# Block-sparse attention and a two-layer MLP: value blocks in every fourth partition, score columns in block-minor order

## The chip, the cores and the metric

The kernel runs on one core of one Trainium2 chip. The metric is device time in microseconds (us): the median of three runs is 771.02, from 770.57 to 773.94. A core has five engines that run their own instruction queues: TensorE (PE in the profile, with weight loads as PEld), VectorE (DVE), ScalarE (ACT), GpSimd (POOL), and SyncE (SP), whose queue issues most DMAs here. Work meets in SBUF, which has 128 partitions, and in PSUM, where PE's results land in eight banks.

## The reference

Four batches, eight heads, 768 positions, head size 64. Positions form 24 blocks of 32. A query block sees the first and the last block, its own and its two neighbours, and three sampled blocks; the query blocks 0 and 23 see everything. The attention's output goes through an MLP with a squared relu.

```python
scores = scale * np.matmul(q, k.transpose(0, 1, 3, 2))
mask = np.abs(blk_i - blk_j) <= window
mask = mask | (blk_i == 0) | (blk_j == 0) | (blk_i == n_blocks - 1) | (blk_j == n_blocks - 1)
for qb in range(n_blocks):
    for kb in sampled_blocks[qb]:
        mask[qb * block:(qb + 1) * block, kb * block:(kb + 1) * block] = True
scores = np.where(mask, scores, -1000000000.0)
...
attn = attn / (np.sum(attn, axis=-1, keepdims=True) + 1e-09)
return np.matmul(attn, v).astype(np.float32)
...
h = x @ w_in
r = np.maximum(h, 0.0)
g = s * (r * r) + b
return (g @ w_out).astype(np.float32)
```

## The kernel before

The kernel has two stages. The attention comes first, the MLP follows on the same core, and the decoding of the MLP's weights (they arrive as 64-bit floats and are split into pairs of 32-bit ones) is spread over the late attention and the early MLP.

**Slots.** The attention runs as a list of slots (`T["ORD"]`, L31). A sparse slot is one query block of two batches with all eight heads: 44 of them, four units each, one unit for each batch and half of the heads. A dense slot has the two query blocks that see everything, for one batch and four heads: 8 of them, two units each. The order is four dense slots, then 18 sparse ones, then four dense ones woven in with sparse ones, then the rest.

**A sparse slot.** The keys are gathered in `keys_tile` (L873): for the slot's window three blocks and the first block, for its samples three blocks and the last one. GpSimd copies them there (`window_k`, `sampled_k`). `scores` (L931) issues 16 matmuls, each in two passes (32 records), on tiles of 64 rows and 32 columns, with the eight key blocks as 256 moving columns, block after block. `maximum` (L954) takes scores out of PSUM, adds a mask per block (`mt`, a column for each of eight blocks) and finds the row's maximum; `exp` (L969) makes exponentials and their sum. `transposes` (L995) turns two chunks of 128 columns, window and samples, so that keys lie on partitions, `evacuate` (L1008) copies them to SBUF, and `av` (L1051) multiplies with values.

**Values.** A value tile has 128 partitions: three blocks of 32 rows and a fourth for the first or last block, one below the other, because the transposed probabilities come out in that order. `window_v` (L769), `sampled_v` (L860) and `global_values` (L757) load them by DMAs of SP, 32 partitions for a block; adjoining blocks go together (`runs`, L747). Window values stay in three streams (A, B, C), in which each slot loads one new block over the oldest; sampled values go round in five places.

**A dense slot.** `scores_dense` (L919) makes 768 columns a unit in two halves of 384. Each half has a maximum (the second begins with the first's), an exponential over 384, four transposes of 96 columns, and an evacuation of 96 partitions to `dense_part` (L729). Where a sparse slot brings window blocks 3n, 3n+1, 3n+2 into a value tile, `av_dense` (L1032) uses their 96 partitions for the dense rows as well. `recip` (L981) adds the sums.

**Tiles that turn.** Probabilities use eight tiles `ptiles` (L287), scores and transposes share six PSUM banks (`next_bank`), `nm` and `dns` hold maxima and sums.

**The order.** `Plan` (L109) simulates the engines with given costs and due times and writes out each engine's order; L1149 to L1315 give it the operations of a slot with their dependences and buffers. PE's own order is a list (`line`, L1306): transposes of a slot, transposed outputs of the slot before, scores of the slot after the next, then the products with values.

Of the kernel before, what the change touches and what calls it, by code (L numbers as in the profile page):

```python
# [9 lines left out]
F32 = mybir.dt.float32  # L10
# [202 lines left out]
def kernel(  # L213
# [73 lines left out]
    ptiles = [cp.tile([P, HALF], F32, tag=f"p{n}", name=f"ptile{n}") for n in range(8)]  # L287
    ps = ctx.enter_context(tc.tile_pool(name="ps", bufs=1, space=PSUM))
# [372 lines left out]
    with ExitStack() as es:  # L661
# [66 lines left out]

        def dense_part(b, x, j, g):  # L729

            n = NCK // 2 * 4 * P
            if ("d", b) not in vbox:
                vbox[("d", b)] = gp.tile([P, 3 * n // 2], F32, tag=f"z{b % 2}", name=f"dp{b}", bufs=1)
            d = vbox[("d", b)]
            if g == 0:
                return d[:, :n].rearrange("p (c u q) -> p c u q", c=NCK // 2, u=4)[:CH, :, 2 * x + j]
            rest = pool("khp" if b % 2 == 0 else "klp")[1].bitcast(F32) if x else d[:, n:]
            return rest.rearrange("p (c u q) -> p c u q", c=NCK // 2, u=2)[:CH, :, j]
# [18 lines left out]
        def global_values(m):  # L757


            value_tiles()  # L760
            if m < 4:
                z, a = "AB"[m // 2], m % 2
                n, j = (NST, 0) if z == "A" else (4, NB - 1)
                nc.sync.dma_start(out=vbox[z][NSL * BLK:, :n, a, :], in_=v[a, j * BLK:(j + 1) * BLK, :].unsqueeze(1).broadcast_to([BLK, n, DM]))
            else:
                nc.sync.dma_start(out=sampled_values(0)[NSL * BLK:], in_=block_rows(0, NB - 1))
                holds["v"].update((row, 0) for row in range(VG))

        def window_v(i, entire, m):  # L769

            _, e, k, r = slots[i]
            rr = runs(k, entire)
            if m < len(rr):
                j, p, n = rr[m]
            else:
                j, p, n = 0, NSL, 1
            nc.sync.dma_start(out=window_values(r)[p * BLK:(p + n) * BLK], in_=block_rows(e, j, n))
# [3 lines left out]
        make_identity(nc, ident)  # L781
        warm = pers.tile([P, 1], F32, name="warm")
# [12 lines left out]
        nc.gpsimd.memset(mt[:, NB - 2, (NB - 1) % 3:(NB - 1) % 3 + 1], NEG)  # L795
# [26 lines left out]
        def sparse_sampled(G):  # L822
# [15 lines left out]
            G.tensor_scalar(out=mt[:, 1:NB - 1, 4:4 + NSL], in0=iv, scalar1=1.0, scalar2=NEG, op0=ALU.min, op1=ALU.mult)  # L838
# [21 lines left out]
        def sampled_v(i, a):  # L860
# [5 lines left out]
            if a == 0 and holds["v"].get(row) != e:  # L866
                holds["v"][row] = e
                nc.sync.dma_start(out=vt[NSL * BLK:], in_=block_rows(e, NB - 1))
# [50 lines left out]
        def scores_dense(i, k):  # L919

            _, b, x, _ = slots[i]
            n, qt, kt = unit_of[i], qts[q_of(i)], kts[b // 2]
            for par in range(2):
                sp = sps[(n + par, k)] = next_bank(f"s{n + par}_{k}")
                for a in range(2):
                    pair = 2 * x + a
                    nc.tensor.matmul(sp[halves[a], :HALF], qt[halves[par], b % 2, pair, halves[a]],
                                     kt[halves[par], k * NB // 2:(k + 1) * NB // 2, b % 2, pair * BLK:(pair + 1) * BLK],
                                     start=True, stop=True, tile_position=(par * D, a * D))

        def scores(i, a):  # L931
# [13 lines left out]
            for par in range(2):  # L945
                to = sps[(u + 2 * a + par, 0)]
                for pair in range(NPAIR):
                    o = (k - 1) % 4 * BLK if k <= 4 * NSP else pair % 2 * D + (k - 1) % 4 * BLK
                    nc.tensor.matmul(to[quads[pair]], qt[halves[par], a, pair, o:o + BLK], keys[halves[par], :, :, pair * BLK:(pair + 1) * BLK],  # L949
# [4 lines left out]
        def maximum(n, g):  # L954
            i, j = units[n]
            kind, b, k, _ = slots[i]
            if g == 0:
                nms[n] = sm.tile([P, 2], F32, tag="nm", name=f"nm{n}", bufs=10)
# [604 lines left out]
```

## Time and profile before

| | us |
|---|---|
| median of three runs | 771.02 |
| lowest, highest | 770.57, 773.94 |
| profiled execution, its own time | 772.56 |
| its span (first to last instruction) | 770.8 |
| granted clock of TensorE, mean | 0.987 |

The profile comes from one execution. Its page gives busy times by engine, the span in 40 slices, DMA queues, a chain of waits followed back from the last instruction, and the costliest groups of instructions. A line of a group reads: source line, engine, operation, written and read tiles, partitions x elements, count | busy time, mean ns of one | idle time of the engine just before, and what ended it. Line numbers are those of the kernel before. The dense groups of before, for instance, are L927 (scores), L966 with `mz` (maxima), L978 with 384 elements (exponentials), L1004 (transposes), and L1017 and L1019 with 96 partitions (evacuations); the sparse ones are L949, L966 with `mt`, L978 with 256, L1006, L1017 and L1019 with 128, L1058 (products with values).

### The profile page before, as it was taken

The page shows a single profiled execution, that of the slowest core. Times are in us where ns is not written, and L with a number is a line of the kernel's source. Part 1 is how long each engine was busy: PE and PEld are TensorE (multiplying, and loading weights), DVE is VectorE, ACT ScalarE, POOL GpSimd, SP SyncE. Part 2 cuts the span into 40 slices and gives each one's busy share as a digit, 9 for nine tenths or more (in the row PEclk, how much of TensorE's full clock was granted, in tenths as well). Part 3 has the DMA queues.
Part 4 walks back from the last instruction along what each step waited for, and adds up shares of the span by engine and source line. Part 5 has one row for each costly group of instructions (what it writes and reads, how often), then busy time and mean ns, then how long its engine had stood idle before and what let it go on. Part 6 is the DMA issues. An engine that isn't in the chain of part 4 may idle for free.

```text
span 770.8 us, 21373 instructions
## 1 busy us (share of the span) xinstructions
PE 733.4 (95%) x8032; PEld 620.6 (81%) x8032; DVE 562.9 (73%) x1433; ACT 473.0 (61%) x1141; POOL 242.1 (31%) x398
## 2 busy tenths in 40 slices
PE   8799787999898999999989999999999999999997
PEld 6477665677667999989878999888898998888896
DVE  4667555988786889888897688697678679666652
ACT  3657565888786877789753444565444467345433
POOL 4846335545430211212032232233222232222221
PEclk9889999999999999999999999999999999999999
DMA  9988987876874535635432222224000022000002
GB/s 241 217 219 225 228 219 200 214 190 188 224 213 122 154 110 152 204 125 155 105 124 86 76 89 69 63 69 123 1 1 1 1 62 83 1 1 0 1 1 82
DMA packets 101110, 89.41 MB, mean 116 GB/s; under 512 B 50192, under 2 KB 79504, under 8 KB 101008
## 3 DMA queue, kind: packets, MB, share of 16 engines
q1 hardware_dynamic: 98704, 81.76, 38.5%
q0 software_dynamic: 2304, 6.29, 3.4%
q8 instruction: 63, 1.03, 0.6%
q14 instruction: 39, 0.32, 0.2%
HBM read 69.15 MB, written 14.68 MB: 109 GB/s over the span
## 4 chain that ended last, share of the span: by engine, by line
PE 77%; DVE 8%; ACT 5%; DMA 4%; issue 3%; SPq 2%; ACTq 0%; DVEq 0%; POOLq 0%; POOL 0%
PE m L617 20%; PE o L481 10%; PE o L482 10%; PE o L480 10%; PE xs L1058 6%; PE s L949 5%; PE t L1006 5%; PE h L438 3%; PE h L440 2%; PE h L439 2%; PE od L1048 2%; PE xs L1070 1%; DMA qr_3s<-in_q_dup_dram 1%; DVE ptile L966 1%; DMA vB<-in_v_dram 1%
## 5 line engine op out<-in xcount | busy, mean ns | idle before, releaser
L459 POOL TENSOR_TENSOR hid<-hid,hid 128x384 fp32r<-128x384 f32 x96 | 105.5, 1100 | 292.8 <-ACT hid L635 255.4
L634 ACT ACTIVATE hid<-hid,sb_b,sb_s 128x384 f32<-128x384 f32 x96 | 68.0, 709 | 152.3 <-DVE hid L628 152.3
L978 ACT ACTIVATE ptile<-ptile,nm 128x256 f32<-128x256 f32 (+1 forms) x208 | 107.2, 518 | 35.7 <-DVE nm L966 35.6
L966 DVE CUSTOM_DVE_ANT_1 ptile<-s,mt 128x256 f32<-128x256 f32 x176 | 64.2, 421 | 30.3 <-PE s L949 29.8
L482 PE MATMUL o<-woutr,hid 128*128 128x512 f32 x168 | 66.4, 395 | 0.0
L481 PE MATMUL o<-woutr,hid 128*128 128x512 f32 x168 | 66.3, 395 | 0.0
L480 PE MATMUL o<-woutr,hid 128*128 128x512 f32 x168 | 65.3, 389 | 0.0
L617 PE MATMUL m<-wout,win 128*128 128x384 f32 x264 | 62.6, 340 | 2.1 <-ACT xrest L1456 1.6
L617 PE MATMUL m<-xp,wop 128*128 128x384 f32 x288 | 58.3, 337 | 0.0
L1058 PEld LDWEIGHTS xs<-vA,pt 128*32 128x32 f32 x1696 | 35.9, 113 | 26.7 <-ACT xst L1075 8.6
L628 DVE SCALAR_TENSOR_TENSOR hid<-hid 128x384 f32<-128x384 f32 x96 | 54.6, 569 | 3.3
L481 PE MATMUL o<-win,hid 128*128 128x512 f32 x144 | 56.8, 395 | 0.0
L617 PE MATMUL m<-xp,win 128*128 128x384 f32 x288 | 55.1, 338 | 1.4 <-DVE xp L601 0.7
L1058 PE MATMUL xs<-vA,pt 128*32 128x64 f32 x1696 | 48.3, 227 | 7.1 <-issue 6.3
L617 PEld LDWEIGHTS m<-xp,win 128*128 128x128 f32 x288 | 51.0, 188 | 4.6 <-DVE xp L601 1.2
L1006 PE MATMUL t<-ident,ptile 128*128 128x128 f32 x352 | 51.5, 287 | 3.0 <-issue 2.5
L635 ACT CAST hid<-hid 128x384 fp32r<-128x384 f32 x96 | 49.4, 514 | 7.5 <-issue 0.4
L617 PEld LDWEIGHTS m<-xp,wop 128*128 128x128 f32 x288 | 51.5, 188 | 2.1
L617 PEld LDWEIGHTS m<-wout,win 128*128 128x128 f32 x264 | 47.4, 188 | 5.1 <-ACT xrest L1456 2.5
L482 PE MATMUL o<-win,hid 128*128 128x512 f32 x126 | 49.8, 395 | 0.0
L480 PE MATMUL o<-win,hid 128*128 128x512 f32 x126 | 49.2, 391 | 0.5 <-ACT ob L486 0.4
L899 POOL COPY kk<-kt 128x256 f32 x132 | 49.0, 409 | 0.0
(187 smaller groups left out, 1829.3 us busy)
## 6 DMA issues: line engine op xcount, KB each, us to landing
vB<-in_v_dram SPq DMA_DIRECT2D x109, 128.0 KB, 4.0
vA<-in_v_dram SPq DMA_DIRECT2D x72, 128.0 KB, 4.2
raw_o<-in_w_out_dram SPq DMA_DIRECT2D x14, 512.0 KB, 3.3
raw_i<-in_w_in_dram SPq DMA_DIRECT2D x12, 512.0 KB, 3.7
xd<-xst SPq DMA_DIRECT2D x44, 128.0 KB, 4.0
out_dram<-ob SPq DMA_DIRECT2D x20, 256.0 KB, 2.0
sum<-xd SPq DMA_DIRECT2D x12, 384.0 KB, 4.0
kt<-in_k_blk_dram SPq DMA_DIRECT2D x8, 384.0 KB, 5.5
```

The lines of the kernel that those rows point to most:

```text
L459: (eng or nc.vector).tensor_tensor(out=htile(5 + i % 3), in0=t, in1=gh.bitcast(F32), op=ALU.subtract)
L480: nc.tensor.matmul(acc, gh[:, tsl], wout(f, 0), start=first, stop=False)
L481: nc.tensor.matmul(acc, gh[:, tsl], wout(f, 1), start=False, stop=False)
L482: nc.tensor.matmul(acc, gl[:, tsl], wout(f, 0), start=False, stop=last)
L617: nc.tensor.matmul(to, w_, x_, start=(c == 0 and k == 0), stop=(c == 1 and k == 2))
L628: vec.scalar_tensor_tensor(out=t, in0=t, scalar=0.0, in1=t, op0=ALU.max, op1=ALU.mult)
L634: nc.scalar.activation(t, t, AF.Identity, bias=sb_b, scale=sb_s)
L635: nc.scalar.copy(gh, t)
L966: nc.vector.tensor_tensor_reduce(out=pt, in0=sp, in1=msk, scale=-scale, scalar=FMAX if g == 0 else nm[:, 0:1], op0=ALU.add, op1=ALU.min, a ...
L978: nc.scalar.activation(pt[:, :w], pt[:, :w], AF.Exp, bias=nms[n][:, last:last + 1], scale=-1.0, accum_out=dns[i][:, g, j:j + 1])
L1006: nc.tensor.transpose(tp[:, (2 * j + c) * P:(2 * j + c + 1) * P], src[:, c * P:(c + 1) * P], ident)
L1058: nc.tensor.matmul(xs[quads[pair]], pt[:, c, quads[pair]], vt[:, a, col:col + D], start=(j == 0 and c == 0), stop=(c == 1), tile_position= ...
```

## The change

A value block's row e goes to partition 4e + p in place of 32p + e, p being the block's place in the tile. All loads of values write every fourth partition, from p on. Three adjoining blocks can no longer go as one run, so the first window of a stream is loaded block by block.

The probabilities must come out in the same order. In a sparse row the 256 columns go from (window or samples, place, element) to (element, place, window or samples): the score matmuls read keys in that order, the mask is repeated over the 32 elements, and a transpose takes every second column. In a dense row, a chunk of 128 columns is 32 elements by four places, of which the fourth is free: scores are written to three of four columns. A unit's 24 blocks make eight such chunks, in pieces of three, three and two, each in a bank and a tile of its own, in place of two halves. Maxima and exponentials run over the three columns of four. The fourth column holds what the tile had before; so the tiles are set to zero once, and the evacuation multiplies by `kept`, which is 0 on every fourth partition and 1 elsewhere. `av_dense` now uses all 128 partitions.

With that, the plan's operations change: a dense slot has three groups of scores of one slot each, six maxima ordered by piece and then unit, six exponentials, six transposed pieces, which take VectorE and ScalarE in turn for evacuation. Its planned costs follow the sizes. At the end the scalings of outputs are put in the order of their transposes.

```diff
     ptiles = [cp.tile([P, HALF], F32, tag=f"p{n}", name=f"ptile{n}") for n in range(8)]
+    for t in ptiles:
+        nc.vector.memset(t, 0.0)
...
+        PIECES = (3, 3, 2)
+
         def dense_part(b, x, j, g):
-            n = NCK // 2 * 4 * P
             if ("d", b) not in vbox:
-                vbox[("d", b)] = gp.tile([P, 3 * n // 2], F32, tag=f"z{b % 2}", name=f"dp{b}", bufs=1)
...
+                vbox[("d", b)] = gp.tile([P, 24 * P], F32, tag=f"z{b % 2}", name=f"dp{b}", bufs=1)
+            if g < 2:
+                return vbox[("d", b)].rearrange("p (c u q) -> p c u q", c=6, u=4)[:, 3 * g:3 * g + 3, 2 * x + j]
+            return pool("khp" if b % 2 == 0 else "klp")[1].bitcast(F32).rearrange("p (c u q) -> p c u q", c=2, u=4)[:, :, 2 * x + j]
...
+        def newcomers(k, entire):
+            return list(range(k - 1, k + 2)) if entire else [newest(k)]
+
         def window_v(i, entire, m):
             _, e, k, r = slots[i]
...
-            nc.sync.dma_start(out=window_values(r)[p * BLK:(p + n) * BLK], in_=block_rows(e, j, n))
+            js = newcomers(k, entire)
+            j, p = (js[m], js[m] % 3) if m < len(js) else (0, NSL)
+            nc.sync.dma_start(out=window_values(r)[p::4], in_=block_rows(e, j))
...
+        kept = pers.tile([P, 1], F32, name="kept")
+        nc.vector.tensor_reduce(out=kept, in_=ident.rearrange("p (r j) -> p r j", j=4)[:, :, :NSL], op=ALU.add, axis=mybir.AxisListType.XY)
...
-            nc.sync.dma_start(out=vt[a * BLK:(a + 1) * BLK], in_=src[bass.ds(j, 1)].rearrange("o e a d -> (o e) a d"))
+            nc.sync.dma_start(out=vt[a::4], in_=src[bass.ds(j, 1)].rearrange("o e a d -> (o e) a d"))
...
+        def piece(y, g):
+            return y[:, :PIECES[g] * P].rearrange("p (c r j) -> p c r j", r=BLK, j=4)[:, :, :, :NSL]
+
-        def scores_dense(i, k):
+        def scores_dense(i, g):
...
+            j0 = sum(PIECES[:g]) * NSL
             for par in range(2):
...
+                to = piece(sp, g).rearrange("p c r j -> p c j r")
                 for a in range(2):
                     pair = 2 * x + a
-                    nc.tensor.matmul(sp[halves[a], :HALF], qt[halves[par], b % 2, pair, halves[a]],
-                                     kt[halves[par], k * NB // 2:(k + 1) * NB // 2, b % 2, pair * BLK:(pair + 1) * BLK],
+                    keys = kt[halves[par], j0:j0 + PIECES[g] * NSL, b % 2, pair * BLK:(pair + 1) * BLK]
+                    nc.tensor.matmul(to[halves[a]], qt[halves[par], b % 2, pair, halves[a]], keys.rearrange("p (c j) r -> p c j r", j=NSL),
...
-                    nc.tensor.matmul(to[quads[pair]], qt[halves[par], a, pair, o:o + BLK], keys[halves[par], :, :, pair * BLK:(pair + 1) * BLK],
+                    nc.tensor.matmul(to[quads[pair]], qt[halves[par], a, pair, o:o + BLK],
+                                     keys[halves[par], :, :, pair * BLK:(pair + 1) * BLK].rearrange("p c j r -> p r j c"),
...
             if kind == "d":
-                pt, sp, msk = pt, sp[:, :HALF], mz.broadcast_to([P, HALF])
+                pt, sp = (piece(y, g).rearrange("p c r j -> p (c r) j") for y in (pt, sp))
+                msk = mz.unsqueeze(2).broadcast_to([P, PIECES[g] * BLK, NSL])
             else:
-                pt, sp = (y[:, :SW].rearrange("p (s e) -> p s e", e=BLK) for y in (pt, sp))
-                msk = mt[:, k].unsqueeze(2).broadcast_to([P, 8, BLK])
+                pt, sp = (y[:, :SW].rearrange("p (r s) -> p r s", s=8) for y in (pt, sp))
+                msk = mt[:, k].unsqueeze(1).broadcast_to([P, BLK, 8])
...
+            pt = piece(pt, g).rearrange("p c r j -> p (c r) j") if kind == "d" else pt[:, :SW]
+            nc.scalar.activation(pt, pt, AF.Exp, bias=nms[n][:, last:last + 1], scale=-1.0,
+                                 accum_out=dns[i][:, 2 * g + j:2 * g + j + 1])
...
-                        nc.tensor.transpose(tp[:CH, c * P:(c + 1) * P], src[:, c * CH:(c + 1) * CH], ident)
+                        nc.tensor.transpose(tp[:, c * P:(c + 1) * P], src[:, c * P:(c + 1) * P], ident)
                     else:
-                        nc.tensor.transpose(tp[:, (2 * j + c) * P:(2 * j + c + 1) * P], src[:, c * P:(c + 1) * P], ident)
+                        nc.tensor.transpose(tp[:, (2 * j + c) * P:(2 * j + c + 1) * P], src[:, c:SW:2], ident)
...
+                if eng == "v":
+                    nc.vector.tensor_scalar(out=o, in0=src, scalar1=kept, scalar2=None, op0=ALU.mult)
+                else:
+                    nc.scalar.activation(o, src, AF.Identity, scale=kept)
+                return
...
-            nu, ng = (2, 2) if kind == "d" else (4, 1)
+            nu, ng = (2, 3) if kind == "d" else (4, 1)
...
+            if dense:
+                for g in range(ng):
+                    for j in range(nu):
+                        n, ms_ = u + j, maxima[j]
+                        o_m = op("v", 560, u + 0.1 * g + T["MP"], lambda n=n, g=g: maximum(n, g), [*s_of[(n, g)], *ms_],
...
+            for g, j in ((g, j) for g in range(ng) for j in range(nu)):
...
-                    on = "va"[(g if dense else j // 2) % 2]
+                on = "va"[(g + j if dense else j // 2) % 2]
...
+        leave = {id(x) for y in tensor.values() for x in y[3]} | {id(x) for y in late.values() for x in y}
+        leave = [o for o in line if id(o) in leave]
+        for prev, o in zip(leave, leave[1:]):
+            o.deps[0].order.append(prev.deps[0])
```

More of the change, by code (lines that the diff above doesn't have):

```diff
@@ L957, in maximum @@
             if g == 0:
-                nms[n] = sm.tile([P, 2], F32, tag="nm", name=f"nm{n}", bufs=10)
+                nms[n] = sm.tile([P, 3], F32, tag="nm", name=f"nm{n}", bufs=10)
             nm, pt, sp = nms[n], next_p(), sps.pop((n, g))
@@ L1199 @@
                 av_deps += globs if e == 0 else []
-                for m in range(len(runs(k, entire)) + (entire and e > 0)):
+                for m in range(len(newcomers(k, entire)) + (entire and e > 0)):
                     pvl = op("s", 450, -8.2 + 0.02 * m if first else u - T["VL"] + 0.1 * m, lambda i=i, w=entire, m=m: window_v(i, w, m), prev[1] if prev else [],
@@ L1213 @@
             s_ops, s_of = [], {}
-            for c in range(2):
+            for c in range(3 if dense else 2):
                 mine = [(u + par, c) for par in range(2)] if dense else [(u + 2 * c + par, 0) for par in range(2)]
@@ L1217 @@
                 new = dense or c == 0
-                deps = [kld[(e // 2, e % 2, p)] for p in range(KPS[e // 2]) if p * 2 // KPS[e // 2] <= c] + lqs[qk][e % 2] if dense else s_deps + lqs[qk][0] + lqs[qk][1]
+                deps = [kld[(e // 2, e % 2, p)] for p in range(KPS[e // 2]) if p * NB // KPS[e // 2] < min(9 * c + 9, NB)] + lqs[qk][e % 2] if dense else s_deps + lqs[qk][0] + lqs[qk][1]
                 o = op("p", cost[0], u, lambda i=i, c=c: scores(i, c), cols=col[0], deps=deps,
@@ new lines @@
+                    for j in range(nu):
+                        n, ms_ = u + j, maxima[j]
+                        o_m = op("v", 560, u + 0.1 * g + T["MP"], lambda n=n, g=g: maximum(n, g), [*s_of[(n, g)], *ms_],
+                                 alloc=[("P", (n, g))] + ([("nm", n)] if g == 0 else []), use=[("B", ("s", n, g))] + ([("nm", n)] if g else []), order=[o_m])
+                        ms_.append(o_m)
+            for g, j in ((g, j) for g in range(ng) for j in range(nu)):
+                n, ms_ = u + j, maxima[j]
+                if not dense:
+                    o_m = op("v", 430, n + T["MP"], lambda n=n: maximum(n, 0), [*s_of[(n, 0)], o_ss],
+                             alloc=[("P", (n, 0)), ("nm", n)], use=[("B", ("s", u + j % 2, 0))], order=[o_m])
+                    ms_.append(o_m)
+                top = g == 0 and j == 0
+                o_e = op("a", 660 if dense else 560, n + T["EP"], lambda n=n, g=g: exp(n, g), ms_,
+                         alloc=[("dn", i)] if top else [], use=[("P", (n, g)), ("nm", n)] + ([] if top else [("dn", i)]), order=[o_e])
+                if dense:
+                    n0, both = n, [o_e]
+                elif j % 2 == 0:
+                    half = o_e
+                    continue
+                else:
+                    n0, both = n - 1, [half, o_e]
+                o = op("p", 470, u, lambda n=n0, g=g: transposes(n, g), both, cols=1024, alloc=[("B", ("t", n0, g))],
+                       use=[("P", (y, g)) for y in range(n0, n + 1)])
+                t_ops.append(o)
+                on = "va"[(g + j if dense else j // 2) % 2]
+                al, us = ([], []) if dense else ([("pt", (n0, g))], [])
+                if dense:
+                    keys = [(f"z{e % 2}", ("dv", e))] if g < 2 else [(f"wp{y}", ("ext", e // 2)) for y in (2, 3)]
+                    al, us = [y for y in keys if y not in held], [y for y in keys if y in held]
+                    held.update(keys)
+                o_ev = op(on, {"a": 560, "v": 640}[on], n + T["EV"],
+                          lambda n=n0, g=g, e=on: evacuate(n, g, e),
+                          [o], alloc=al, use=[("B", ("t", n0, g)), *us], order=[o_ev])
+                if dense:
+                    devs.setdefault(e // 2, []).append(o_ev)
+                for y in range(n0, n + 1):
+                    evs.setdefault(y - u, []).append(o_ev)
```

82 lines of the change are left out of this document (20 added, 62 removed).

## The prediction

> **What bounds the kernel now.** I read the page's head first, then the table of stages, then the chain of waits.
>
> ```profile
> span 770.8 us, 21373 instructions
> ## 1 busy us (share of the span) xinstructions
> PE 733.4 (95%) x8032; PEld 620.6 (81%) x8032; DVE 562.9 (73%) x1433; ACT 473.0 (61%) x1141; POOL 242.1 (31%) x398
> ```
>
> TensorE is busy for 95% of the span, but that is a mean over two different halves. The windows view separates them (columns: stretch, its length, busy time of PE, PEld, DVE, ACT and POOL with instruction counts, granted clock, DMA share, GB/s).
>
> ```profile
> 25.00:40.00 15.00, 11.23 (x120) 5.36 (x120) 7.28 (x30) 7.72 (x27) 10.14 (x24) 0.78 1.06 215
> 40.00:125.00 85.00, 77.07 (x2278) 58.91 (x2278) 54.27 (x229) 55.01 (x190) 36.79 (x92) 0.96 0.83 216
> 125.00:160.00 35.00, 30.07 (x551) 20.18 (x548) 27.15 (x101) 25.89 (x81) 18.19 (x38) 0.95 0.90 226
> 160.00:246.00 86.00, 78.67 (x2347) 59.21 (x2331) 68.65 (x266) 69.23 (x221) 32.45 (x78) 0.98 0.69 187
> 246.00:400.00 154.00, 151.16 (x814) 135.01 (x811) 131.03 (x237) 119.74 (x218) 29.80 (x30) 1.00 0.47 142
> ```
>
> Attention ends near 246 us. After that comes the MLP, where PE is busy 151.2 of 154 us; the change touches nothing there. Whatever it does, it does before 246 us, where the DMA engines are 69 to 106% busy, PE has 3.8 + 7.9 + 4.9 + 7.3 = 23.9 us of idle time from 25 us on, and the granted clock is below 1. The chain of waits (start, us, what) says what these gaps are; its first line here is the share by line between 40 and 246 us.
>
> ```profile
> by line: PE xs L1058 21.2%; PE s L949 19.4%; PE t L1006 18.0%; PE od L1048 8.3%; issue 7.6%; PE xs L1070 5.0%; DVE ptile L966 4.7%; PE t L1004 2.7%; DMA vB<-in_v_dram 2.5%; PE s L927 2.4%; DVE pt L1017 1.5%; ACT ptile L978 1.4%; DVE xss L10
> ```
> ```profile
> 28.89 10.21 DMA qr_3s<-in_q_dup_dram
> ...
> 76.77 2.03 issue
> ...
> 82.61 2.28 issue
> ...
> 106.52 1.78 issue
> ...
> 118.49 1.45 PE s L927 x16
> ...
> 123.30 1.02 PE s L949 x32
> ...
> 126.83 5.05 DMA vB<-in_v_dram
> ...
> 200.24 2.52 issue
> ...
> 408.80 2.10 PE m L617 x12
> ```
>
> So the sparse part is a PE queue with three kinds of holes: queries that land late at the start (10.2 us), one transfer at 127 us (5.1 us), and pieces of "issue" (8.6 us in the four shown), in which PE waited for nothing that the profile shows.
>
> **The change, part by part.**
>
> *Value loads.* Each value block is written to 32 partitions. Before, they adjoin; after, they lie four apart over all 128.
>
> ```profile
> 26.00:31.00 5.00, 4.33 (x36) 2.46 (x28) 2.74 (x12) 1.09 (x4) 5.00 (x12) 0.66 1.06 216
> ...
> 300.00:320.00 20.00, 20.00 (x103) 18.21 (x102) 18.23 (x35) 16.96 (x31) 4.82 (x5) 1.00 0.64 204
> ```
> ```profile
> vB<-in_v_dram SPq DMA_DIRECT2D x109, 128.0 KB, 4.0
> ...
> raw_i<-in_w_in_dram SPq DMA_DIRECT2D x12, 512.0 KB, 3.7
> ```
>
> Between 26 and 31 us, when the first value blocks come in, engines that are busy all the time move 216 / 1.06 = 204 GB/s. Between 300 and 320 us, when weights go to all 128 partitions, they move 204 / 0.64 = 319 GB/s per full share. A value load of 128 KB takes 4.0 us to land, a weight load of four times the size 3.7 us. I estimate that spread value blocks move at the second rate, that is in 204 / 319 = 64% of the time. The bounds are nothing (the two rates may differ for another reason, such as sizes and sources) and the whole 36%. I take most of it, since the slow rate stands at the place where value blocks dominate.
> The Trainium skill, "SBUF — State Buffer", section on Door 1 (the DMA port swizzle), gives a reason: 32 adjoining partitions reach half of the 16 ports, measured there at 189 GB/s against 328 for all. The two rates here lie close to these, but no run so far shows a spread value block.
>
> What that is worth on the path:
> - Start: the queries that PE awaits at 28.9 us share the engines with value loads. If two thirds of what is ahead of them are values, 10.2 x 2/3 x 0.36 = 2.5 us go. Next late would be PE itself with the dense transposes.
> - 126.83: VectorE stands in order before a weight load that shares the engines with values; the same piece lands in 3.7 us at four times the size later, so at most 5.05 - 3.7 = 1.4 us go. I take 1.4.
> - "issue": 7.6% of 206 us is 15.7 us, most of it unavoidable small change. The four long ones (8.6 us) stand where DMA is 83% busy; the profile doesn't say that DMA causes them. Bounds 0 and 8.6; I take about half, 4.1, as they are rare where DMA is quiet.
> Sum: -8.0 us, bounds 0 and -15.
>
> *More, smaller value loads.* A stream's first window comes block by block: over the three streams 9 loads in place of 4 for each of the two pairs of batches, 10 issues more. SP issues each in some 0.4 us and they carry the same bytes; what stands behind them on SP's queue are sampled values and spills needed later. I cost them at nothing; without that cover it would be 4 us.
>
> *Sparse slots.* The columns of a score row are permuted. Counts, columns and bytes stay: 44 slots, each with one group of 32 score matmuls (1.02 us). 0 us if a strided read costs nothing: a rival below. The maximum reads the mask in runs of 8 in place of one value repeated: 0, at most 44 x 4 x (550 - 421) ns = 23 us of VectorE time by the rows below. The transposes take every second column as their weights: 0, and if that slowed them by what rival 1 assumes, as much again as there.
>
> *Dense slots* (8, each 2 units). Per unit, two maxima and two exponentials over 384 become three over 288, 288 and 192. The eight transposes remain eight, in three banks. The evacuations go from two to three, with a factor per partition.
>
> ```profile
> L978 ACT ACTIVATE ptile<-ptile,nm 128x256 f32<-128x256 f32 x176 | 87.7, 502 | 22.8 <-DVE nm L966 22.7
> L634 ACT ACTIVATE hid<-hid,sb_b,sb_s 128x384 f32<-128x384 f32 x96 | 68.0, 709 | 152.3 <-DVE hid L628 152.3
> ...
> L966 DVE CUSTOM_DVE_ANT_1 ptile<-s,mt 128x256 f32<-128x256 f32 x176 | 64.2, 421 | 30.3 <-PE s L949 29.8 <-issue 0.5
> ...
> L978 ACT ACTIVATION_READ_ACCUMULATOR ptile<-ptile,nm 128x1 f32 x208 | 39.6, 190 | 0.0
> ...
> L978 ACT ACTIVATE ptile<-ptile,nm 128x384 f32<-128x384 f32 x32 | 19.5, 611 | 12.8 <-DVE nm L966 12.8
> ...
> L966 DVE DVE_READ_ACCUMULATOR2_ANT nm<- 128x1 f32 x208 | 17.3, 83 | 0.0
> ...
> L1075 ACT COPY xst<-xs 128x256 f32<-128x256 f32 x44 | 16.3, 371 | 10.6 <-PE xs L1070 10.6
> ...
> L1017 DVE COPY dp<-t 96x512 f32<-96x512 f32 x16 | 10.4, 678 | 0.3 <-PE t L1004 0.2
> L966 DVE CUSTOM_DVE_ANT_0 ptile<-s,mz,nm 128x384 f32<-128x384 f32 x16 | 9.9, 618 | 2.3 <-DVE nm L966 0.3 <-PE s L927 0.3 <-PE t L1004 0.2
> L966 DVE CUSTOM_DVE_ANT_0 ptile<-s,mz 128x384 f32<-128x384 f32 x16 | 8.8, 550 | 5.7 <-PE s L927 5.5
> ...
> L1019 ACT COPY dp<-t 96x512 f32<-96x512 f32 x8 | 4.5, 572 | 0.8 <-PE t L1004 0.7
> L990 DVE RECIPROCAL rc<-rc 128x2 f32<-128x2 f32 x8 | 1.3, 166 | 0.3
> ```
>
> - VectorE, maxima: (550 - 421) / 128 = 1.0 ns a column. So 454, 522 and 426 ns and 3 x 83: 1651 ns against 550 + 618 + 2 x 83 = 1334; +0.63 us a slot.
> - VectorE, evacuations: at 1 ns a column from 678, three of a slot (550, 422, 550) against two (1356): +0.17. One more addition before the reciprocal: +0.17. In all +0.97 us a slot, 7.8 us for eight.
> - ScalarE, exponentials: (611 - 502) / 128 = 0.85 ns a column; 529 + 529 + 448 + 3 x 190 = 2076 against 1602: +0.95 us a slot.
> - ScalarE, evacuations: (572 - 371) / 256 = 0.79 ns a column, so 471 for 384 and 371 for 256. The factor from a tile I price at 709 - 611 = 98 ns (a scale from a tile against none). 569 + 569 + 469 = 1607 against 1144: +0.46. In all +1.4 us a slot, 11.3 us for eight.
> - PE: passes over 288 and 192 columns carry the same total as over 384; 16 passes of 384 columns, four at a time, take 1.45 us, about 1 ns a column, as 32 of 256, eight at a time, do in 1.02. 0 us.
> The first four slots lie ahead of the wait for queries (28.9 us), which takes up their 4 to 6 us: I cost them at nothing, and at 4 us if that wait went altogether. The last four lie between 125 and 160 us, where ScalarE has 9.1 and VectorE 7.9 us free out of 35. ScalarE gets 4 x 1.4 = 5.7 us more. I take 3.5 us on the path, since the order there alternates between the engines and a later first exponential delays PE; bounds 0 and 10.
>
> *At the head:* eight memsets and one reduction on VectorE, some 4 us by the copy above at 1 ns a column or less. VectorE has nothing to do before the list of sampled blocks lands; 0, at most 1 us.
>
> Sum: -8.0 + 3.5 = -4.5 us. The profiled execution took 772.56 us (span 770.8 and 1.8 around it) and becomes 768.1. It lies 1.5 above the median, so against 771.02 I forecast **766.5 us**, own range 761 to 770.
>
> **The rivals.**
> 1. *Strided score reads* (the other side, slower). In the sparse scores, PE now reads keys at r, j, c: neighbouring columns lie 4 KB or 1 KB apart, before 32 in a row. A pass takes 1 ns a column, while the MLP's takes 2.10 us / 12 / 384 = 0.46 ns with the same 4 bytes. So a strided read may be up to 2.2 times slower than the fastest seen before it decides; past that, every slot pays. If it ran at a quarter of the fast rate, 1.8 ns, the 44 groups would cost 44 x 1.02 x 0.83 = 37 us more: 766.5 + 37 = 803.5. Against it: the margin of 2.2. For it: up to four such streams read the same partitions at once. 17%.
>    The Trainium skill, same page (SBUF "cachelines", under Door 1), has lines of 16 bytes that need at least two hits for full rate; here each column hits another line. At half the fast rate, 0.91 ns, it would still hide under 1 ns; its size for this case isn't given there.
> 2. *The transfers were hidden anyway*: the long "issue" pieces are not the DMA's doing and the queries wait for their own bytes. Then 771.0 - 1 + 3.5 = 773.5. For it: only 4 + 10 us of the chain carry a DMA's name. 22%.
> 3. *Dense slots cost more*: a slot's scores now take all 6 rotating banks and 6 of 8 probability tiles (4 and 4 before), and every exponential of a unit waits for three maxima. Their scores are also written in steps of four columns; at twice the time the four late slots would pay 4 x 2 x 1.45 = 11.6 us. If these slots pay 13 in place of 3.5 us: 776. 13%.
> 4. *All gaps close*, clock included: -15 + 3.5, 759.5. 10%.
>
> **How the numbers follow.** My forecast gets 38%. The range reaches from 757 to 804, with the first rival's price in it; I leave out some 15%, most of it above. A measurement can tell about 0.5% here, 3.9 us. Faster by more: most of the forecast (0.32) and rival 4 (0.10), 0.42. Within: the rest of the forecast (0.06), most of rival 2 (0.19) and a part of 3 (0.03), 0.28. Slower: 0.30.
>
> **What would show it.** Value loads should land in 3 us or less and the DMA share between 40 and 125 us fall from 0.83 to some 0.65. The long "issue" pieces should thin out. A group of 32 sparse score passes should stay at 1.02 us; if it doesn't, rival 1 holds. Exponentials should read 529 and 448 ns. The first MLP matmul should start before
>
> ```profile
> 246.54 0.44 PE L438 MATMUL h<-xp,win 128*128 128x384 f32 x1 [0.32 <-ACT pt L1019]
> ```
>
> by about 4.5 us. If the DMA share falls and this start doesn't move, rival 2 is right.

## The result, and the profile after

| | us |
|---|---|
| before, median (range) of four runs beside it | 772.48 (770.57 to 776.07) |
| after, median (range) of four runs | 810.68 (809.46 to 817.06) |
| ratio, 95% interval | 1.0505 [1.0435, 1.0576] |
| profiled execution after, its span | 809.77, 808.0 |

The forecast was 766.5. The kernel became 38 us slower, and the range of 757 to 804 did not hold the time.

The windows view of the kernel after, with the same stretches as before (stretch, length, busy time of PE, PEld, DVE, ACT, POOL with counts, granted clock, DMA share, GB/s):

```profile
40.00:125.00 85.00, 85.00 (x1956) 51.74 (x1945) 46.34 (x204) 49.34 (x170) 29.57 (x75) 1.00 0.66 194
125.00:160.00 35.00, 31.05 (x645) 21.00 (x638) 24.14 (x99) 24.80 (x86) 16.46 (x37) 1.00 0.72 203
160.00:246.00 86.00, 80.62 (x1728) 48.46 (x1726) 55.81 (x222) 57.50 (x177) 31.10 (x72) 0.98 0.53 154
```

Before, PE had 7.9 us without work in the first stretch; now it has none. It is not faster, though: it has fewer instructions there (1956 against 2278), so each lasts longer. The timeline of PE names the one that does (start, us):

```profile
122.67 0.38 PE L1088 MATMUL xs<-ident,xss 128*128 128x128 f32 x2
122.99 2.32 PE L958 MATMUL s<-kk,qr_2s 64*32 64x256 f32 x32
...
283.29 0.42 PE L440 MATMUL h<-xp,win 128*128 128x384 f32 x1
```

A group of 32 sparse score passes takes 2.3 us where it took 1.02. The first MLP matmul starts at 283.29 in place of 246.54, 36.8 us late, which is nearly the whole loss; the MLP behind it is as before. The chain of waits between 40 and 125 us has no transfer in it any more:

```profile
by line: PE s L958 45.2%; PE t L1019 23.1%; PE xs L1076 19.8%; PE od L1066 7.6%; PE xs L1088 4.4%
```

The signs that I had named for faster transfers are there too. The DMA share fell from 0.83 to 0.66 (0.65 was forecast), and value loads land in 3.2 and 3.0 us (median, last column) where they took 4.0 and 4.2:

```profile
vB<-in_v_dram SPq DMA_DIRECT2D x109, 128.0 KB, 3.2
vA<-in_v_dram SPq DMA_DIRECT2D x88, 128.0 KB, 3.0
```

So two questions follow. Are the strided reads of the keys the whole cause? And why did loads that land sooner bring nothing?

### The profile page after: what moved, and what is told of

The parts are those of the page before. It is cut to its first block, busy times and chain, and to the rows that moved or that the text cites. A ratio compares the mean times of both kernels' runs of the same rounds, so it can differ in the third digit from the quotient of the medians.

```text
span 808.0 us, 21671 instructions
## 1 busy us (share of the span) xinstructions
PE 780.2 (97%) x8096; PEld 626.7 (78%) x8096; DVE 571.8 (71%) x1490; ACT 483.3 (60%) x1181; POOL 242.5 (30%) x398
## 3 DMA queue, kind: packets, MB, share of 16 engines
q8 instruction: 64, 1.05, 0.5%
## 4 chain that ended last, share of the span: by engine, by line
PE 80%; DVE 8%; ACT 6%; issue 2%; DMA 2%; SPq 1%; POOL 1%; ACTq 0%; DVEq 0%
PE m L619 19%; PE s L958 12%; PE o L483 9%; PE o L484 9%; PE o L482 9%; PE t L1019 6%; PE xs L1076 5%; PE h L440 2%; PE h L442 2%; PE h L441 2%; PE od L1066 2%; ACT ptile L990 2%; PE xs L1088 1%; DVE ptile L977 1%; PE t L1017 1%
## 5 line engine op out<-in xcount | busy, mean ns | idle before, releaser
L990 ACT ACTIVATE ptile<-ptile,nm 128x256 f32<-128x256 f32 (+2 forms) x224 | 112.8, 509 | 75.8 <-DVE nm L977 75.7
L1076 PEld LDWEIGHTS xs<-vA,pt 128*32 128x32 f32 x1696 | 33.5, 109 | 44.9 <-issue 26.0
L891 POOL COPY kk<-kt 128x256 f32<-128x256 f32 (+2 forms) x46 | 20.5, 449 | 128.1 <-PE s L958 128.0
L1019 PE MATMUL t<-ident,ptile 128*128 128x128 f32 x352 | 54.7, 298 | 0.0
L1019 PEld LDWEIGHTS t<-ident,ptile 128*128 128x128 f32 x352 | 46.1, 208 | 6.3 <-ACT ptile L990 2.2
```

Of the source, the lines that this page charges most:

```text
L990: nc.scalar.activation(pt, pt, AF.Exp, bias=nms[n][:, last:last + 1], scale=-1.0, accum_out=dns[i][:, 2 * g + j:2 * g + j + 1])
L1019: nc.tensor.transpose(tp[:, (2 * j + c) * P:(2 * j + c + 1) * P], src[:, c:SW:2], ident)
L1076: nc.tensor.matmul(xs[quads[pair]], pt[:, c, quads[pair]], vt[:, a, col:col + D], start=(j == 0 and c == 0), stop=(c == 1), tile_position= ...
```

## The experiments

The theory at the start was that the strided reads cost 44 x 1.25 = 55 us of TensorE and that the rest of the change gave 17 us back. Its rivals were that the permuted order costs as such, writes to PSUM included, and that the steps cost only together with the new places of the values. That reads and spread values each cost something was not among them. In what follows, "kernel 1" is the kernel of experiment 1, and so on.

**1. Strided writes in place of strided reads.** A sparse pass reads the keys in a row again and writes its scores to PSUM in steps of eight columns; the output stays the same.

```diff
-matmul(to[quads[pair]], q..., keys[..., pair * BLK:(pair + 1) * BLK].rearrange("p c j r -> p r j c"),
+matmul(to[quads[pair]].rearrange("p (r j c) -> p c j r", j=4, c=2), q..., keys[..., pair * BLK:(pair + 1) * BLK],
```

> The changed kernel with one edit: the sparse scores read their keys in a row as before and PSUM takes them in steps of 8 columns, so that the same order comes out. Theory (reading keys in steps costs 44 groups x (2.27 - 1.02) us = 55 us, and all the rest of the change gains some 17): a group of 32 score passes is back at 1.02 to 1.06 us and the time at about 756, at most 765 if holes come back that the longer groups covered. Rival (the price lies in the permuted order as such, PSUM's side included): groups stay near 2.2 us and the time near 810.

Measured: 801.54 (801.02 to 803.56), ratio 1.0385 [1.0361, 1.0409]. The groups are fast again, as the timeline of PE shows, yet the kernel is only 9 us faster than the kernel after, and the expectation of 756 to 765 fell.

```profile
148.64 1.09 PE L958 MATMUL s<-kk,qr_2s 64*32 64x256 f32 x32
```

In the list of waits of PE a new one stands on top (engine, line, releaser: us in total, times, longest), and the chain from 40 to 125 us now goes through it:

```profile
PE xs L1076 <- DMA vA<-in_v_dram: 21.7, 10, 5.1
```
```profile
by line: DMA vA<-in_v_dram 22.7%; PE xs L1076 16.1%; PE t L1019 15.8%; PE s L958 11.0%; PE od L1066 6.3%; PE xs L1088 2.8%; DVE ptile L977 0.9%; PE s L937 0.7%; issue 0.7%; DVE nm L977 0.0%
```

**2. Strided reads alone.** The kernel before, whose sparse passes read keys in the new order and write the scores to the old places (in steps of 128 columns).

```diff
-matmul(to[quads[pair]], q..., keys[halves[par], :, :, pair * BLK:(pair + 1) * BLK],
+matmul(to[quads[pair]].rearrange("p (c j r) -> p r j c", j=4, c=2), q...,
+       keys[halves[par], :, :, pair * BLK:(pair + 1) * BLK].rearrange("p c j r -> p r j c"),
```

> The kernel before with one edit: the sparse scores read keys in steps, as the changed kernel does, and PSUM takes them at the old places. Theory: groups of 2.2 to 2.3 us; PE idle time takes up a part of 55 us, so 815 to 828. Rival (the steps cost only together with the new layout of values): groups near 1.02 and 772.

Measured: 801.43 in one run, less than the 815 to 828 expected. More runs of the same kernel:

> The same kernel as e2_before_read_strided, timed in three rounds: 800 to 803 if its one run was typical; 806 to 811 if it was not, and then the strided reads alone are the whole of the change's price.

Measured: 803.39 (801.24 to 804.48), ratio 1.0409 [1.036, 1.0458]. The reads alone cost 31 us. That is less than 55, in the main because TensorE lost idle time as well; the windows of this kernel in the later run:

```profile
40.00:125.00 85.00, 83.62 (x1974) 50.51 (x1978) 46.82 (x205) 48.99 (x169) 32.32 (x80) 0.99 0.78 202
125.00:160.00 35.00, 34.74 (x671) 21.73 (x655) 27.26 (x96) 25.35 (x77) 17.19 (x37) 1.00 0.85 205
```

Before, PE was idle for 7.9 and 4.9 us in these two; here for 1.4 and 0.3. Over the whole span its busy time grew by 44 us (733.4 to 777.2) and the span by 30, so some 14 us went into holes. The score passes alone take 53 us more (54.5 to 107.1, summed over their groups); the others take some 9 less. The granted clock was higher here, 0.99 and 1.00 against 0.96 and 0.95, which may be why; no run tests it.

**3. Values in adjoining partitions.** Kernel 1, with the value blocks in 32 adjoining partitions. The values then stand at places that the probabilities don't match, so that part of the output is another; the work is the same.

```diff
-nc.sync.dma_start(out=window_values(r)[p::4], in_=block_rows(e, j))
+nc.sync.dma_start(out=window_values(r)[p * BLK:(p + 1) * BLK], in_=block_rows(e, j))
...
-nc.sync.dma_start(out=vt[a::4], in_=...)
+nc.sync.dma_start(out=vt[a * BLK:(a + 1) * BLK], in_=...)
```

> The kernel e1 with value blocks in 32 adjoining partitions again, by the same number of loads (values then meet the probabilities of other keys: the product with values is not the reference's). If the spread over all partitions is what gains: value loads land in 4 us again, the DMA share between 40 and 125 us is above 0.8, and the time is 8 to 17 us above e1. If the other edits gain (order of maxima, order of scalings, pieces): within 3 us of e1.

Measured: 775.73 (771.11 to 778.49), ratio 1.0031 [1.0005, 1.0057]. So, with fast score passes, spreading the values costs 26 us, the opposite of my forecast, and neither branch of the expectation came. Why? As a group the loads don't take longer to land: their median is 3.1 us for vA in kernel 1 and 4.1 here. What differs is how long SyncE takes to issue one. The line of the window loads in kernel 1 (duration of one issue in ns, min/median/max) and here:

```profile
L778 SPq DMA_DIRECT2D vA<-in_v_dram x59: 598/616/1691, 16.1 to 270.6; - x59
```
```profile
L778 SPq DMA_DIRECT2D vA<-in_v_dram x59: 311/382/1672, 15.4 to 247.0; - x59
```

And the timeline of SyncE's queue, first in kernel 1, then here (start, us, line, x issues in the piece):

```profile
61.47 0.53 SPq L1100 DMA_DIRECT2D xd<-xst  x1
62.05 0.42 SPq L697 DMA_DIRECT2D kt<-in_k_blk_dram  x1
62.57 1.27 SPq L778 DMA_DIRECT2D vA<-in_v_dram  x1
64.16 2.39 SPq L874 DMA_DIRECT2D vB<-in_v_dram  x3
66.64 0.79 SPq L1100 DMA_DIRECT2D xd<-xst  x1
67.48 0.42 SPq L697 DMA_DIRECT2D kt<-in_k_blk_dram  x1
68.00 0.63 SPq L778 DMA_DIRECT2D vA<-in_v_dram  x1
68.94 3.21 SPq L874 DMA_DIRECT2D vA<-in_v_dram  x3
72.25 0.53 SPq L1100 DMA_DIRECT2D xd<-xst  x1
```
```profile
61.05 0.37 SPq L1100 DMA_DIRECT2D xd<-xst  x1
...
65.20 0.38 SPq L1100 DMA_DIRECT2D xd<-xst  x1
65.63 0.42 SPq L697 DMA_DIRECT2D kt<-in_k_blk_dram  x1
66.43 1.88 SPq L874 DMA_DIRECT2D vB<-in_v_dram  x3
68.41 0.37 SPq L778 DMA_DIRECT2D vA<-in_v_dram  x1
```

There is one spill (L1100) to a slot. In kernel 1 the pieces stand nearly end to end, and from spill to spill it takes 5.2 and 5.6 us; here 4.2, with room between. On the average from 40 to 125 us the turn takes 5.1 us in kernel 1 and 4.5 here; if all 44 slots differ by that, it is some 25 us. My reading is that a window load is issued late, behind three sampled loads of 0.8 us or more each. These lines alone don't show it: the four window loads on the chain of kernel 1 took 3.7 to 6.1 us from the start of their issue, so they were among the slower ones too. Experiments 4 and 5 test it. The Trainium skill, "Perfetto Trace Analysis", section "What 'DMA-bound' means", names this case: the issuing engine's sequencer can be the limit, seen as a track of solid DMA slices, and that window is descriptor generation, not data movement. The trace agrees: SyncE's pieces in kernel 1 have almost no room between them while the DMA engines are 66% busy. Why a spread destination doubles the time of an issue, no run shows.

**4. Two issues for one.** Kernel 3 (nothing spread), each value load issued in two of 64 KB. That doubles the suspected cost without the spread.

```diff
+for y in range(2):
-    nc.sync.dma_start(out=vt[a * BLK:(a + 1) * BLK], in_=...)
+    nc.sync.dma_start(out=vt[a * BLK:(a + 1) * BLK, y], in_=...)
```

> As e3_values_adjoin (values in adjoining partitions, strided score writes; the same wrong places of the values), but each of the 59 window loads and 132 sampled loads is issued as two loads of 64 KB, one for each batch row; bytes, packets and places stay. Theory 'SyncE issues too slowly': in e1 an issue of a value load took 0.60 to 0.62 us against 0.32 to 0.38 in e3, and SyncE was issuing for 86% of 40 to 125 us against 74%; two issues of some 0.3 us take as long as one spread issue, so the time goes from 775.7 up to e1's 801.5 or more: 794 to 815, with waits of TensorE for vA at the value products as in e1. Rival 'the spread destination itself is slow to fill': nothing is spread here, 772 to 781.

Measured: 859.58 (856.45 to 861.12), ratio 1.111 [1.1057, 1.1163]. The direction and the wait are those of the theory (PE waits 51.4 us for vA), the size is not, 860 in place of 794 to 815: I had counted the issues alone. The queue shows why it is more:

```profile
65.22 0.42 SPq L1102 DMA_DIRECT2D xd<-xst  x1
65.96 4.19 SPq L876 DMA_DIRECT2D vB<-in_v_dram  x6
70.25 0.83 SPq L779 DMA_DIRECT2D vA<-in_v_dram  x2
71.14 0.42 SPq L697 DMA_DIRECT2D kt<-in_k_blk_dram  x1
71.64 0.42 SPq L1102 DMA_DIRECT2D xd<-xst  x1
```

Six sampled issues take 4.19 us, 0.7 each, although one issue alone is 0.32: the register work for a sampled block's address stands between them and is doubled too. This slot takes 6.4 us of SyncE.

**5. The window loads on another queue.** Kernel 1 (spread, slow issues), with its 59 window loads issued by GpSimd.

```diff
-nc.sync.dma_start(out=window_values(r)[p::4], in_=block_rows(e, j))
+nc.gpsimd.dma_start(out=window_values(r)[p::4], in_=block_rows(e, j))
```

> As e1_write_strided (spread values, scores written in steps), but the 59 window loads of values are issued by GpSimd instead of SyncE. Theory 'SyncE issues too slowly': 59 x 0.62 = 36 us of issuing leave SyncE, which is about what spreading the 132 sampled loads added (132 x 0.28 = 37), GpSimd has room (14 of 40 us busy with copies): the time falls from 801.5 to 766 to 782. Rival 'the spread destination itself is slow to fill': the loads are the same, 795 to 806.

Measured: 775.69 (771.11 to 780.02), ratio 1.003 [0.9997, 1.0063]. The same spread destinations, issued by two engines, and the 26 us are gone. The wait for vA has left the list of PE's waits; spill to spill takes 4.1 us on SyncE here, and 4.6 on the average from 40 to 125 us:

```profile
61.51 0.53 SPq L1100 DMA_DIRECT2D xd<-xst  x1
...
65.66 0.53 SPq L1100 DMA_DIRECT2D xd<-xst  x1
```

The window loads themselves did not get faster: their median landing is 3.5 us, where it was 3.1 in kernel 1. So the spread costs time by SyncE's issuing, not by the transfers.

**6. The spills on ScalarE.** Kernel 1, with the spills taken from SyncE in place of the window loads.

```diff
-nc.sync.dma_start(out=xd[b, hf, :, m]..., in_=xst)
+nc.scalar.dma_start(out=xd[b, hf, :, m]..., in_=xst)
```

> As e1_write_strided, but the 44 spills of a sparse slot's output are issued by ScalarE, right behind the copy that makes them. Theory 'SyncE issues too slowly': 44 x 0.53 = 23 us and the waits for ScalarE's copies (14 us in e1) leave SyncE; ScalarE gets half a us a slot on 3.6 of 4.9: 775 to 793. Rival 'the spread destination itself is slow to fill': 798 to 808, ScalarE's issues only add.

Measured: 804.71 (801.09 to 808.34), two runs. A miss: the theory had 775 to 793, and the time lies in the rival's range. SyncE was relieved of 44 issues but shows new waits of its own, for the landing of those spills:

```profile
SPq L778 <- DMA xd<-xst: 13.8, 6, 5.1
SPq L874 <- DMA xd<-xst: 13.7, 9, 3.5
```

27 us of waiting replace the 23 of issuing; why a value load waits for a spill, I did not find out. So this run does not support the theory. It does not refute it either, since the queue of SyncE was not relieved in the end; the case rests on experiments 4 and 5.

**7. Is SyncE a limit in the kernel before, or still in kernel 5?** The kernel before with its window loads on GpSimd, and kernel 5 with the third sampled load of each slot on GpSimd as well.

```diff
-nc.sync.dma_start(out=window_values(r)[p * BLK:(p + n) * BLK], in_=block_rows(e, j, n))
+nc.gpsimd.dma_start(out=window_values(r)[p * BLK:(p + n) * BLK], in_=block_rows(e, j, n))
```
```diff
-nc.sync.dma_start(out=vt[a::4], in_=...)
+(nc.gpsimd if a == 2 else nc.sync).dma_start(out=vt[a::4], in_=...)
```

> The kernel before, with its window loads issued by GpSimd instead of SyncE. If SyncE's issuing limits the kernel before too (24.7 us of issues in 40 to 80 us, 62%), it gains like e7 against e1, on a smaller scale: 758 to 768. If SyncE has room enough there, as the theory has it (its queue stands at 71% with the register work, and the limit bites above some 85%): 768 to 776.

> As e7_windows_pool, and of the three sampled value loads of a slot the third is issued by GpSimd too. If SyncE still limits e7 (83% of 40 to 80 us): 760 to 771, under the kernel before. If e7 is bound elsewhere (the vector engines' part of the dense slots and TensorE itself): 772 to 779.

Measured: 774.43 (771.63 to 779.3), ratio 1.0017 [0.9986, 1.0048], and 779.41 (777.17 to 782.32), ratio 1.0097 [1.0065, 1.013]. No to both: where SyncE has room, taking loads from it brings nothing, and with two loads a slot on GpSimd its own key copies come late (PE waits 5.0 us for one). No version here beats the kernel before.

**8. How far may a read stride?** The kernel after, with each sparse pass split into two of 128 columns. Stream A (queries qr_0s, qr_1s) reads keys in a row, stream B (qr_2s, qr_3s) every second column (8 bytes), stream C (qr_4s, qr_5s) every fourth (16 bytes).

```diff
+y = (1, 2, 4)[r]
+for c in range(2):
-matmul(to[quads[pair]], q..., keys[...].rearrange("p c j r -> p r j c"),
+    matmul(to[quads[pair]].rearrange("p (x y j c) -> p c j y x", y=y, j=4, c=2)[:, c], q...,
+           keys[...].rearrange("p c j (x y) -> p c j y x", y=y)[:, c],
```

> The changed kernel with each sparse score matmul split in two of 128 columns, and keys read in steps that differ by stream: 1 column in stream A (queries qr_0s, qr_1s), 2 columns (8 bytes) in B (qr_2s, qr_3s), 4 columns (16 bytes) in C (qr_4s, qr_5s). If a read in steps costs by lines of 16 bytes that need two hits: groups (64 passes) of 1.02 us in A and B and 2.2 in C. If any step costs: B lies between. If only the long steps of the changed kernel cost: all three near 1.02.

Measured: 814.5 in one run. Groups of 64 half passes of streams A, B and C from the timeline:

```profile
64.39 1.47 PE L960 MATMUL s<-kk,qr_0s 64*32 64x128 f32 x64
69.11 1.53 PE L960 MATMUL s<-kk,qr_3s 64*32 64x128 f32 x64
74.31 2.37 PE L960 MATMUL s<-kk,qr_4s 64*32 64x128 f32 x64
```

A half pass carries half the columns with a weight load of its own, so a group in a row takes 1.47 us here and not 1.02, that is 1.44 ns a column (64 passes of 128 columns, eight side by side). Steps of 8 bytes add next to nothing to that (1.53 us); a read that takes up to 1.4 ns a column would not show. Steps of 16 bytes take 2.37 us, 2.3 ns a column: as much as the long steps of the kernel after (2.3 us for as many columns). The Trainium skill, "SBUF — State Buffer", under Door 1, has lines of 16 bytes that want at least two hits each for full rate. The trace agrees: the price is there at one hit a line (16 bytes) and not seen at two (8 bytes).

**9. Does a strided pass pay by itself?** Kernel 1, whose dense passes read keys in steps of 1 KB. Four of them run side by side, of the sparse ones eight.

```diff
-matmul(to[halves[a]], q..., keys.rearrange("p (c j) r -> p c j r", j=NSL),
+matmul(to[halves[a]].rearrange("p c j r -> p c r j"), q..., keys.rearrange("p (c j) r -> p c r j", j=NSL),
```

> As e1_write_strided, but the dense score passes read the keys in steps of 1 KB (the sparse ones stay as they are), four passes at a time on a quarter of the array each, where the sparse ones have eight. If a strided read costs the pass itself (2.2 ns a column whatever runs beside it): a dense group of 24 passes goes from 1.53 us to 3.3, over 16 units of three groups. If it costs a budget that the eight concurrent passes share (about 0.28 ns a column each), four passes stay under it and the groups remain at 1.5 to 1.7.

Measured: 797.66 in one run. The third and the fourth dense slot in the timeline of this kernel, then of kernel 1 (start, us, for 24 passes):

```profile
18.25 2.10 PE L937 MATMUL s<-kt,qr_0d 64*64 64x288 f32 x24
23.83 1.99 PE L937 MATMUL s<-kt,qr_0d 64*64 64x288 f32 x24
```
```profile
18.63 1.57 PE L937 MATMUL s<-kt,qr_0d 64*64 64x288 f32 x24
23.77 1.53 PE L937 MATMUL s<-kt,qr_0d 64*64 64x288 f32 x24
```

At a granted clock of 1.00 in both, the strided group takes 2.0 to 2.1 us, 1.3 times as long. That is neither the 3.3 us of a price for each pass nor the 1.5 to 1.7 of a budget that four passes stay under. The means over all dense passes (527 against 500 ns) hide it, because the first dense slots of kernel 1 ran at a granted clock of 0.76 and those of this kernel at 1.00. A sparse pass, with eight side by side, goes from 382 to 697 ns, and its group from 1.02 to 2.3 us. So a strided read costs more where more passes read side by side; what they share, no run shows. (The dense tiles are also twice as wide, and their steps shorter, 1 KB against mostly 4 KB and more; these were not told apart.)

**10. What of the 38 us is what?** The reads alone make 803.4, the kernel after 810.7. Three runs on the 7 us between them: the kernel after with its window loads on GpSimd; with transposes that take 128 adjoining columns as weights (`src[:, c * P:(c + 1) * P]` for `src[:, c:SW:2]`; the probabilities then meet other values); and with values in adjoining partitions (the edit of experiment 3; the values stand at other places).

> The kernel after, with its window loads issued by GpSimd instead of SyncE. Theory 'two causes': the strided reads remain (29 us in e2 alone) and SyncE's share of the 38 goes: 798 to 806, e2's 801.4 with some 2 for the dense slots. Rival 'in the kernel after the reads alone set the time, SyncE costs nothing any more': 808 to 813.

> The kernel after, but a sparse slot's eight transposes take 128 adjoining columns of the probabilities as weights in place of every second one (the probabilities then meet other value rows: that part of the output is another). Theory 'TensorE sets the end of the attention stage, every us of its work counts': the group of eight goes from 1.15 back to 1.02 us, 44 x 0.13 = 5.7 us, so 803 to 807 where the kernel after has 810.5. Rival 'the 9 us between e2 and the kernel after come from the dense slots or the value loads': 809 to 812.

> The kernel after with the value blocks in 32 adjoining partitions (as in e3, so the values stand at other places and that part of the output is another); the strided reads stay. If the 9 us over e2 are the slow issues of spread loads: 799 to 804. If they are the dense slots and the other edits: 808 to 813.

Measured: 810.37 (809.6 to 810.68), ratio 1.0488 [1.0436, 1.054]; 813.8 (812.73 to 816.02), ratio 1.0556 [1.0504, 1.0609]; 810.08 (808.64 to 810.71), ratio 1.0494 [1.0448, 1.0541]. Neither the queue nor the spread counts in the kernel after: TensorE is busy all the time from 40 to 125 us there, and SyncE's longer issues are hidden behind it. The transposes' weights don't account for the 7 us either; that expectation (803 to 807) fell. Their cost is real and went away, from the kernel after (first line) to this one (second),

```profile
L1019 PE MATMUL t<-ident,ptile 128*128 128x128 f32 x352 | 54.7, 298 | 0.0
```
```profile
L1019 PE MATMUL t<-ident,ptile 128*128 128x128 f32 x352 | 48.5, 281 | 0.0
```

but the time did not fall: a wait of 4.8 us of a dense transpose for VectorE's maxima took its place between 125 and 160 us (on the chain, VectorE itself waits 4.8 us there for a load of vB). What is left for the 7 us is the dense slots and the other edits together; I did not separate them.

## Why the prediction was wrong, step by step

- **Sparse slots, "0 us if a strided read costs nothing"**: this step failed first. The term was put at nothing because of "the margin of 2.2" between a pass's 1 ns a column and the 0.46 ns of the MLP's passes; but those read in a row, one at a time on the whole array (128*128), and say nothing of eight strided passes side by side. Rival 1 was right, with 17%, and its price too low: not 1.8 but 2.2 ns a column (2.29 us / 1024 columns). I priced 37 us; it is 55 us of TensorE's time, of which 31 reach the end when nothing else changes (experiment 2). "For it: up to four such streams read the same partitions at once" was the sentence that mattered, as experiment 9 suggests: four passes side by side pay 1.3 times, eight pay 2.2 times.
- **Value loads, "spread value blocks move ... in 64% of the time"** fell as well. In the kernel after, a fully busy set of DMA engines would move 194 / 0.66 = 294 GB/s, and with the values adjoining (experiment 10) 278:

```profile
40.00:125.00 85.00, 85.00 (x1944) 51.69 (x1941) 46.49 (x204) 49.38 (x170) 29.52 (x75) 1.00 0.68 189
```

  That is 6% more, not 56%. My 204 GB/s came from one crowded stretch at the start, my 319 from another kind of load. In that stretch the spread did raise the rate, by how much the two pairs of kernels don't agree: 243 / 0.83 = 293 GB/s in kernel 1 against 241 / 1.05 = 230 in kernel 3, with adjoining values,

```profile
25.00:40.00 15.00, 13.47 (x270) 9.09 (x266) 12.88 (x56) 14.11 (x51) 14.01 (x34) 1.00 0.83 243
```
```profile
25.00:40.00 15.00, 12.13 (x218) 8.19 (x224) 12.48 (x51) 12.72 (x45) 14.06 (x33) 1.00 1.05 241
```

  but 283 in the kernel after against 269 with adjoining values (experiment 10). So the transfers can be faster where the engines are full, but that did not set the time: kernels 3 and 5, without and with the spread, both take 775.7 us. The rule of the Trainium skill that I cited beside it (half of the ports for 32 adjoining partitions) did not show as a sooner landing: the landings fell to 3.2 and 3.1 us with adjoining values too (experiment 10). That they fell because the slots got longer and the engines had less to do at once is the likely reason; it was not tested.
- So two of my own signs, landings of 3 us and a DMA share of 0.65, came true for the wrong reason: with adjoining values they read 3.1 to 3.2 us and 0.68. That is luck. The third, a score group at 1.02 us, is the one that told.
- **"Issue" and the wait at 126.83, -5.5 us**: no gain at the end. With adjoining values (kernel 3) PE's value products wait 10.0 us for "issue", with spread ones issued in time (kernel 5) only 1.5; but there the transposes wait 12.7 us for VectorE's maxima, where it was 7.3, and the time is the same. (Of the four long pieces, the one at 200.24 us stood where the DMA share was 0.69, not 0.83.) **Start, -2.5 us**: no gain that holds. The first value product starts at 40.2 us before, at 36.2, 37.4 and 38.8 in kernels 1, 3 and 5, and at 39.2 in the kernel after both with spread and with adjoining values (experiment 10), so not by where the values lie.
- **More loads, "SP issues each in some 0.4 us", cost at nothing**: the 10 more loads were not the point. I counted new issues and did not ask whether the some 190 old ones get longer: 0.32 to 0.38 us became 0.60 to 0.62. Hidden in the kernel after, this step alone costs 26 us as soon as the keys are read in a row again (experiments 1, 3 and 5). It is a rival that I did not have.
- **Rival 2**, "the transfers were hidden anyway", at 773.5: with both faults taken away (kernel 5, 775.7) this is what is left. Rival 4's gaps did close between 40 and 125 us in the kernel after (PE 85.0 of 85 us, clock 1.00), but because the passes got longer; no run shows that they close for another reason.
- **Dense slots, +3.5 us**: near, though not measured alone. Kernel 3, which has all edits but the spread and the strided reads, is 2.4 us over the kernel before (0.4 to 4.4). The sizes, from the groups by form of the kernel after: exponentials 551 and 456 ns (529 and 448 forecast), maxima 452, 513 and 414 (454, 522, 426), VectorE's evacuations 610 where I had 550:

```profile
L990 ACT ACTIVATE ptile<-ptile,nm 128x288 f32<-128x288 f32 x32 | 17.3, 551 | 15.3 <-DVE nm L977 15.3
L977 DVE CUSTOM_DVE_ANT_1 ptile<-s,mz,nm 128x288 f32<-128x288 f32 x16 | 7.7, 513 | 1.5 <-ACT ptile L990 1.4
L1027 DVE TENSOR_SCALAR dp<-t,kept 128x384 f32<-128x384 f32 x16 | 9.7, 610 | 0.0
```

  Dense scores written to three of four columns cost nothing, as costed: 24 passes take 1.46 to 1.58 us on the chain between 125 and 160 us, 16 longer ones took 1.45. Where TensorE is the bound, the same edits may stand with up to 7 us; they were not taken apart.
- **Maxima, reading the mask in runs of 8**: nothing, as costed; they stay at 421 ns.
- **Transposes with every second column**: costed at 0, they were 0.13 us a group of eight, 6 us of TensorE in all, of which no run showed a us at the end.

## What to carry to other kernels

Before a change of layout, list every operand whose step in memory it changes, on the reading side of TensorE first, and count how many passes read side by side: that is where this one was decided. Price a DMA on both ends, the transfer and its issue, and draw up the time that the issuing queue needs for one turn of the loop beside that of the busiest engine. A sign that would also come about by the kernel just getting slower (a lower DMA share, sooner landings) is no evidence for a forecast.

## What the runs showed of the hardware that was not expected

- Moving operands of 4 bytes, eight passes side by side: 1.0 ns a column in a row, 2.3 in steps of 16 bytes and 2.2 to 2.3 in steps of 1 KB and more. Steps of 8 bytes took no more than 1.5, where a row took 1.44 in the same short passes. With four passes side by side, steps of 1 KB took 1.3 times as long as a row.
- Scores written to PSUM with gaps took no longer than in a row: 382 ns a sparse pass in kernel 1 (steps of eight) as before; the dense passes write three of four.
- An issue of a 128 KB load by SyncE takes 0.60 to 0.62 us if its 32 rows go to every fourth partition, 0.32 to 0.38 if they go to adjoining ones; GpSimd issues the spread ones in 0.55.
- Weights taken from every second column: 208 ns a load in the kernel after, against 141 for adjoining columns in experiment 10 and 144 in the kernel before.
